# Attention, a dense layer and eight experts in one kernel: the last routing by halves and pairs, conversions behind the selection, contiguous copies of transposed queries and keys

## The chip, the cores and the metric

The kernel runs on one core of a Trainium2 chip. The time is the device time of one execution in microseconds, as the median of several runs. The profile is one execution recorded by the hardware profiler; times in it count from the first instruction of the core.

## The reference

Three stages follow one another: causal attention with a window of 64, a dense layer with a gated activation, and eight experts of which each token takes at most one.

```python
def reference(...):
    # attention: q, k, v of (4, 8, 576, 64); rel = query - key position
    scores = where((rel >= 0) & (rel < 64), q @ k.T / sqrt(64), -1e9)
    attn = softmax(scores) @ v
    x = attn.transpose(0, 2, 1, 3).reshape(2304, 512)
    # dense layer, w_in 512 x 2048, w_out 2048 x 512
    h = x @ w_in
    x = (h * tanh(softplus(h))) @ w_out
    # experts: 8, w1 512 x 1024, w2 1024 x 512
    keep = x @ w_skip > 0
    logits = x @ w_gate
    e = argmax(logits); gate = softmax(logits)[e]
    y = gate * (relu(x @ w1[e]) @ w2[e])
    return where(keep, x + y, x)
```

## The kernel before

The 2304 tokens are six blocks (`m`) of 384, each three tiles (`t`) of 128. The program has two parts, and in each a planner (`Plan`) orders tasks by costs, due times and buffer counts that are written into the code, and then emits them; within such a region every engine issues in the order of emission. `rounds` is emitted at the end of the first region, behind all its tasks. Where the instructions of one region fall among those of the other on the same engine is left to a scheduler.

The first part does the attention in 24 pairs of heads (`pr`), the dense layer in 96 chunks (`L1`, activation, `L2`), and the routing of each block. For the first eight pairs queries and keys are loaded in their natural layout, four rows to a partition, and transposed on TensorE (`nat_T`, line 437) into PSUM; `nat_k` and `nat_q` copy them to SBUF (helper `copy`, lines 317 on ScalarE and 319 on VectorE), with a step of four words in what they write.

The routing of a tile: `xe` copies the tile out of PSUM and negates it (lines 830, 832), `rT` transposes it (843), `re` copies the transposes, `rl` forms the logits (873), and a `Group` of tiles goes through some 15 small VectorE instructions: maximum, one-hot, the place among the tokens of an expert (`place` on TensorE), the row in the experts' buffer (`keep`, line 946), sum, gate, tag, and the running count `cum`. Blocks 0 to 4 form a group of three tiles; the last block has three groups of one. `scatter` then writes the tokens to the experts' rows in DRAM.

For the last block expert 0 doesn't wait for DRAM: `pick_mat` (line 1093) makes a selection matrix of 0 and 1 from the rows, `select` (1099) multiplies it with the tile split in two parts (`xs_H`, `xs_L`), and `sel_H` copies the selected tokens of each half of the features to SBUF (`xgH`). `rounds` (1147 to 1160) then computes from the counts the value `nrounds` and, for each expert, `level`, which says how many of its places are taken.

In the second part TensorE does for each expert `E1` in four steps (`fp`, line 1222) with two PSUM buffers, which `h_H` (1249) and `h_L` (1255, VectorE) read, then `E2` (1266), between its steps the transposes of the next expert's tokens (`xg_T`, 1208), and at the end `E2_second`. Before the fourth step of `E1` TensorE reads `level` into a register (`load_over`). SyncE reads `nrounds` (line 1432, at the end of the code).

The weights of the experts' second layer are loaded as f32 (`el`, line 333) and split into a rounded part (`eH`, a cast) and a remainder (`eL`, line 343, a subtraction on VectorE). The first 32 weight tiles are handled in the first part, as the dense weights in their places are used up; their staging buffers (`cv`) are two. The last four of the 32 are tiles j = 4 to 7 of expert 2. `keep_warm` (1176) fills TensorE's planned waits in the first part with matmuls without use.

Of the kernel before, what the change touches and what calls it, by code (L numbers as in the profile page):

```python
# [9 lines left out]
F32 = mybir.dt.float32  # L10
# [12 lines left out]
N1 = 144  # L23
# [148 lines left out]
def tile_kernel(  # L172
# [37 lines left out]
    def ctile(shape, dt, name):  # L210
        return cst.tile(shape, dt, tag=name, name=name)
# [42 lines left out]
    G.iota(iota8, pattern=[[NE, CAP]], base=0, channel_multiplier=0)  # L254
    first_t = []
    for n in (1, 1, 1, 3):
        t = ctile([128, n, NE + 1], F32, f"first{len(first_t)}")
        G.memset(t, 0.5)
        first_t.append(t)
    nslot = [0]  # L260
# [80 lines left out]
    def expert_L(eng, key):  # L341
# [21 lines left out]
    BUFS = dict(ps=3, ph=2, po0=1, po1=1, po2=1, rk=4, rq=2, vt=3, kT=2, qT=2, P=2, PT=2, xHL=2,  # L363
                cv=2, ca=2, u=3, gHL=2, xs=3, xf=1, grp3=1, grp1=3, lqs=1)
    plan = Plan(BUFS)
# [63 lines left out]
    def nat_T(pr, i):  # L429
        t = nat[pr][i]  # L430
        nr = nat[pr][2] if i else 96
        if pr < 4:
            o = ps_o.tile([128, 4, 128], F32, tag=f"po{i}", name="tqk")
        else:
            o = ps_s.tile([128, 4, 128], F32, tag="ps", name="tqk")
# [391 lines left out]
    def x_evac(eng, m, t):  # L827
# [6 lines left out]
        G.tensor_copy(xs[:, DM + 1:XW].bitcast(I32), tok[:, n:n + 1])  # L834

    def x_store(m, t):
        n = 3 * m + t
        SP.dma_start(out=out[128 * n:128 * n + 128, :], in_=xs_t[m, t][:, :DM])
# [6 lines left out]
    def route_Te(eng, m, t):  # L845
        if m == NB - 1:
            xf = rqp.tile([128, NK, 128], F32, tag="rk", name="xf", bufs=4)
        else:
            xf = sml.tile([128, NK, 128], F32, tag="xf", name="xf", bufs=1)
        copy(eng, xf, xf_t[m, t])  # L850
        xf_t[m, t] = xf

    def route_few(m, t):
# [16 lines left out]
    def route_lg(m, t):  # L870
        lp_t[m, t] = lp = ps_s.tile([128, NE + 1], F32, tag="ps", name="lp")
        for kk in range(NK):
            PE.matmul(lp, xf_t[m, t][:, kk], wgs[:, kk, :NE + 1], start=kk == 0, stop=kk == NK - 1)
# [5 lines left out]
    class Group:  # L879


        def __init__(self, m, t0, n):
            self.m, self.t0, self.n, self.i = m, t0, n, 3 * m + t0

        def lg(self):
            if self.n == 1:
                return lp_t[self.m, self.t0].rearrange("p (n c) -> p n c", n=1)
            return lg_t[self.m]

# [3 lines left out]
        def small(self, w, name, dt=F32):  # L893
            return sml.tile([128, self.n, w], dt, tag=f"{name}{self.n}", name=name, bufs=3 if self.n == 1 else 1)

# [17 lines left out]
        def first(self):  # L913
            self.f = first_t[self.t0 if self.n == 1 else 3]
            V.scalar_tensor_tensor(self.f[:, :, :NE], self.z, 0.0, self.d, op0=ALU.is_ge, op1=ALU.mult)
# [81 lines left out]
    for m in range(NB):  # L997
# [3 lines left out]
        for t in range(3):  # L1001
            T(("xe", m, t), two(.48, .6), lambda e, m=m, t=t: x_evac(e, m, t), after=[("L2t", NF * m + NF - 1, t) if last else ("L2", NF * m + NF - 1)],
              get=[("xs", ("xs", m, t))], use=[("po", m, t)], due=tb + 2)
            T(("xo", m, t), one(SS, .45), lambda e, m=m, t=t: x_store(m, t), after=[("xe", m, t)], lat=2.5,
              due=tb + 20, use=[("xs", m, t)])
            T(("rT", m, t), one(PP, .43), lambda e, m=m, t=t: route_T(m, t), after=[("xe", m, t)] + [("re", m, t - 1)] * (t > 0),
              get=[("ps", ("rtp", m, t))], due=tb + dt * (2 + 2 * t), use=[("xs", m, t)])
            T(("re", m, t), two(.48, .6), lambda e, m=m, t=t: route_Te(e, m, t), after=[("rT", m, t)],
              get=[("rk" if last else "xf", ("xf", m, t))], use=[("rtp", m, t)])
            if not last:  # L1010
# [4 lines left out]
                continue  # L1015
            T(("rl", m, t), one(PP, .75), lambda e, m=m, t=t: route_lg(m, t), after=[("re", m, t), ("wg",)],
              get=[("ps", ("lp", m, t))], use=[("xf", m, t)], due=tb + dt * (3 + 2 * t))
# [4 lines left out]
        prev = None  # L1022
        for t0, n in ([(t, 1) for t in range(3)] if last else [(0, 3)]):
            g = Group(m, t0, n)
            lgs = [("lg", m) if n > 1 else ("rl", m, t0)]
            lu = [("lp", m, t0)] if n == 1 else []
            key = lambda x, m=m, t0=t0: (x, m, t0)
# [3 lines left out]
            def R(name, eng, cost, fn, after, use=(), late=0.0, get=(), lat=None, g=g, gb=gb, td=td):  # L1031
# [21 lines left out]
            for t in range(n):  # L1053
# [60 lines left out]
    for t in range(3):  # L1114
        T(("sH", t), two(.52, .34), lambda e, t=t: xs_H(e, t), after=[("xe", L, t)],
          get=[("xHL", "xsHL")] if t == 0 else (), use=[("xs", L, t)], due=te + 10 + t, behind=[("sH", t - 1)] * (t > 0))
        T(("sL", t), one(VV, .6), lambda e, t=t: xs_L(e, t), after=[("sH", t)], use=[("xs", L, t)],
          due=te + 12 + t)
        T(("pm", t), one(VV, .2), lambda e, t=t: pick_mat(t), after=[("ke", L, t)], get=[("kT", ("pick", t))] if t != 1 else (), use=[("pick", 0)] if t == 1 else (),
          behind=[("pm", t - 1)] * (t > 0), due=te - 3 + .1 * t)  # L1120
# [12 lines left out]
    for n in range(32):  # L1133
# [3 lines left out]
        if key[1] < NK:  # L1137
# [79 lines left out]
    def E1(e, fp):  # L1217
        ph_t[e, fp] = ph = pl1.tile([128, 2, N1], F32, tag="ph2", name="ph2")
        for i in range(2):
            f = 2 * fp + i  # L1220
            for kk in range(NK):
                PE.matmul(ph[:, i], w1_t[e, kk][:, 128 * f:128 * f + 128], xgT[e][:, kk, :N1],  # L1222
                          start=kk == 0, stop=kk == NK - 1)

# [241 lines left out]
```

## Time and profile before

| | us |
|---|---|
| median of 3 runs | 688.57 (687.44 to 689.02) |
| the profiled execution, its own time | 686.42 |
| its span, first to last instruction | 684.60 |
| TensorE busy (matmuls) | 669.3 |
| VectorE busy | 460.5 |
| ScalarE busy | 410.2 |
| GpSimd busy | 60.0 |

The engines are PE (TensorE; PEld its weight loads), DVE (VectorE), ACT (ScalarE), POOL (GpSimd) and SP (SyncE; SPq its issues). A matmul's end is modelled, so a busy TensorE is not one at its peak, and the matmuls of `keep_warm` count as busy. A row of a timeline gives the start in us, the duration in us, engine, line, operation, output<-inputs, shape and count, and in brackets how long the engine was idle before and what released it. A row of a window gives the stretch, its length, the busy us (and instructions) of PE, PEld, DVE, ACT and POOL, the granted TensorE clock as a share of 2.4 GHz, the busy share of the DMA engines, and GB/s. A row of a group gives line, engine, operation, shapes and count, then the busy us and the mean ns of one, then the idle time before. Loads are told by the minimum, median and maximum time from issue to landing in us.

### The profile page before, as it was taken

How to read it: one execution, taken by the hardware profiler on the slowest of the kernel's cores; microseconds unless marked ns; L12 is line 12 of the kernel's file. 1: busy time of each engine (PE TensorE's matmuls, PEld its weight loads, DVE VectorE, ACT ScalarE, POOL GpSimd, SP SyncE). 2: the span in 40 equal slices, each digit the busy share in tenths (PEclk: the TensorE clock that was granted, in tenths of full speed). 3: DMA queues.
4: the chain of work that ended last, by engine and by line, in shares of the span. 5: the costliest groups of instructions: out<-in, count | busy, mean ns of one | idle time of the engine just before them, and what ended most of it. 6: DMA issues, size and time to landing. Idle time of an engine off the chain costs nothing. (4 is left out here: it accounts for less than half of the span.)

```text
span 684.6 us, 13449 instructions
## 1 busy us (share of the span) xinstructions
PE 669.3 (98%) x4870; PEld 574.7 (84%) x4870; DVE 460.5 (67%) x1298; ACT 410.2 (60%) x994; POOL 60.0 (9%) x114
## 2 busy tenths in 40 slices
PE   7999999999999999999999999999999999999995
PEld 6787766788888888988888888898888888998983
DVE  4999999876666555565776656566678574685352
ACT  5999778677667775776555565456554253543241
POOL 3000000000010001000020001100020122211141
PEclk9999999999999999999999999999999999999998
DMA  9999966877432312232220100044564677588300
GB/s 203 284 323 315 245 128 135 200 152 158 78 75 46 81 35 56 47 93 50 51 60 13 58 1 11 18 152 139 155 178 167 227 255 249 208 281 294 142 18 28
DMA packets 150493, 92.54 MB, mean 135 GB/s; under 512 B 111869, under 2 KB 128253, under 8 KB 150416
## 3 DMA queue, kind: packets, MB, share of 16 engines
q1 hardware_dynamic: 147696, 87.11, 47.1%
q0 software_dynamic: 2720, 4.42, 1.7%
q8 instruction: 46, 0.75, 0.5%
q14 instruction: 31, 0.25, 0.1%
HBM read 73.96 MB, written 17.86 MB: 134 GB/s over the span
## 5 line engine op out<-in xcount | busy, mean ns | idle before, releaser
L737 PE MATMUL ph<-xH,w 128*128 128x384 f32 x768 | 220.6, 348 | 0.2
L788 PE MATMUL po<-w,gH 128*128 128x512 f32 x480 | 154.3, 402 | 0.0
L737 PEld LDWEIGHTS ph<-xH,w 128*128 128x128 f32 x768 | 140.9, 188 | 7.0 <-issue 1.7
L737 PE MATMUL ph<-xL,w 128*128 128x384 f32 x384 | 130.0, 338 | 0.0
L745 ACT ACTIVATE u<-u 128x384 f32<-128x384 f32 x96 | 50.3, 524 | 121.2 <-DVE u L742 121.2
L788 PEld LDWEIGHTS po<-w,gH 128*128 128x128 f32 x480 | 87.2, 188 | 17.2 <-issue 1.6
L788 PE MATMUL po<-w,gL 128*128 128x512 f32 x240 | 95.0, 396 | 0.0
L764 DVE SCALAR_TENSOR_TENSOR u<-u,ph 128x384 f32<-128x384 f32 x80 | 44.1, 551 | 68.0 <-ACT u L758 67.6
L737 PEld LDWEIGHTS ph<-xL,w 128*128 128x128 f32 x384 | 72.2, 188 | 4.0 <-issue 2.2
L1222 PEld LDWEIGHTS ph<-xgT,w 128*128 128x128 f32 x512 | 63.9, 190 | 1.5 <-DVE xgT L319 0.4
L1222 PE MATMUL ph<-xgT,w 128*128 128x144 f32 x512 | 64.7, 287 | 0.4 <-DVE xgT L319 0.3
L742 DVE TENSOR_SCALAR u<-ph 128x384 f32<-128x384 f32 x96 | 53.2, 554 | 14.8 <-PE ph L737 13.7
L773 DVE TENSOR_TENSOR gL<-u,gH 128x384 fp32r<-128x384 f32 x80 | 44.5, 557 | 17.1 <-ACT gH L317 14.2
L531 ACT ACTIVATE P<-P,mx 128x128 f32<-128x128 f32 x144 | 55.6, 390 | 0.1
L788 PEld LDWEIGHTS po<-w,gL 128*128 128x128 f32 x240 | 45.1, 188 | 10.8
L749 ACT ACTIVATE u<-u 128x384 f32<-128x384 f32 x96 | 50.4, 525 | 2.9
L758 ACT ACTIVATE u<-u 128x384 f32<-128x384 f32 x96 | 50.2, 523 | 2.3
L755 ACT ACTIVATE u<-u 128x384 f32<-128x384 f32 x96 | 50.1, 522 | 2.3
L788 PE MATMUL po<-w,g 128*128 128x512 f32 x96 | 44.0, 594 | 0.0
L343 DVE TENSOR_TENSOR w<-st,w 128x512 fp32r<-128x512 f32 x64 | 42.6, 683 | 0.6
L1266 PE MATMUL po<-w,hH 128*128 128x512 f32 x128 | 42.6, 414 | 0.0
L279 POOL DMA_INDIRECT xg_d<-xs,r_si x18 | 18.6, 1031 | 234.4 <-DVE gH L319 74.3
(166 smaller groups left out, 966.8 us busy)
## 6 DMA issues: line engine op xcount, KB each, us to landing
st<-in_moe_w_dram SPq DMA_DIRECT2D x64, 256.0 KB, 5.9
w<-in_moe_w_dram SPq DMA_DIRECT2D x32, 512.0 KB, 5.2
w<-in_moe_w_in_dram SPq DMA_DIRECT2D x16, 512.0 KB, 6.3
w<-in_moe_w_out_dram SPq DMA_DIRECT2D x16, 512.0 KB, 6.3
out_dram<-xs SPq DMA_DIRECT2D x18, 256.0 KB, 2.4
xg<-xg_d SPq DMA_DIRECT2D x16, 257.0 KB, 3.8
ca<-w SPq DMA_DIRECT2D x16, 256.0 KB, 3.2
xg_d<-nothing SPq DMA_DIRECT2D x16, 256.0 KB, 4.9
```

Of the source, the lines that this page charges most:

```text
L343: eng.tensor_tensor(l, raw_w.pop(key), h.bitcast(F32), op=ALU.subtract)
L531: A.activation(P[:, i], P[:, i], AF.Exp, bias=mx[:, 0, u % 2, i:i + 1], scale=-1.0, accum_out=mx[:, 1, u % 2, i:i + 1])
L737: PE.matmul(phs[c], a[:, kk], b[:, kk], start=kk == 0 and n == 0, stop=kk == NK - 1 and n == len(terms) - 1)
L742: V.tensor_scalar(u, phs[c], 20.0, None, op0=ALU.min)
L745: A.activation(us[c], us[c], AF.Exp)
L749: A.activation(us[c], us[c], AF.Square, bias=1.0)
L755: A.activation(us[c], us[c], AF.Ln, scale=0.5, bias=half_t[c])
L758: A.activation(us[c], us[c], AF.Exp, scale=-1.0)
L764: V.scalar_tensor_tensor(o, us[c], 1.0, phs[c], op0=ALU.subtract, op1=ALU.mult)
L773: eng.tensor_tensor(gL, us[c], gH.bitcast(F32), op=ALU.subtract)
L788: PE.matmul(po[m, t], a[:, ts], b, start=f == 0 and n == 0, stop=f == NF - 1 and n == len(terms) - 1)
L1222: PE.matmul(ph[:, i], w1_t[e, kk][:, 128 * f:128 * f + 128], xgT[e][:, kk, :N1], start=kk == 0, stop=kk == NK - 1)
```

## The change

Four things change. The transposes of queries and keys are written to PSUM with a step of four words, so that the copies out of it are contiguous on both sides. In the last block the third tile's two copies (`xe`, `re`) are split into a half on VectorE and a half on ScalarE. Tiles 0 and 1 of that block are routed as a group of two, tile 2 as a group of one, whose places count the first group's one-hot rows directly and so don't wait for `cum`. Other work is ordered behind: `sl`, `sm` (and with it `ep`, `ga`, `tg`) and `co` behind the last selection matrix, `sL` of tiles 1 and 2 behind the third tile's copies, and `eH` of expert 2's tiles behind both selection copies, which are now fixed to one on ScalarE and one on VectorE. The first step of `E1` of expert 0 goes through the first half of the features for both outputs before the second.

```diff
-    for n in (1, 1, 1, 3):
+    for n in (1, 2, 3):
...
-            o = ps_o.tile([128, 4, 128], F32, tag=f"po{i}", name="tqk")
+            o = ps_o.tile([128, 128, 4], F32, tag=f"po{i}", name="tqk")
...
-            PE.transpose(o[:, r, :nr], t[:nr, r].rearrange("p j d -> p (j d)"), ident[:nr, :nr])
+            PE.transpose(o[:, :nr, r], t[:nr, r].rearrange("p j d -> p (j d)"), ident[:nr, :nr])
...
-            copy(eng, kT[:, c0 + pad:c0 + pad + nk].rearrange("p (a r) -> p r a", r=4), tqk[pr, 1][:, :, r0:r0 + nk // 4])
+            copy(eng, kT[:, c0 + pad:c0 + pad + nk], tqk[pr, 1][:, r0:r0 + nk // 4].rearrange("p a r -> p (a r)"))
...
-        copy(eng, qk_tiles(pr)[0].rearrange("p (a r) -> p r a", r=4), tqk[pr, 0][:, :, :96])
+        copy(eng, qk_tiles(pr)[0], tqk[pr, 0][:, :96].rearrange("p a r -> p (a r)"))
...
+    def x_evac_half(eng, m, t, n):
...
+        hs = slice(256 * n, 256 * n + 256)
+        if eng is A:
+            A.activation(xs_t[m, t][:, hs], po[m, t][:, hs], AF.Copy, scale=-1.0)
+        else:
+            V.tensor_scalar(xs_t[m, t][:, hs], po[m, t][:, hs], -1.0, None, op0=ALU.mult)
...
+    def route_Te_half(eng, m, t, n):
...
+        copy(eng, xf[:, 2 * n:2 * n + 2], p[:, 2 * n:2 * n + 2])
...
-                for t2 in range(t):
-                    PE.matmul(pp[:, t], ones8, self.oh[:, t2], start=False, stop=False)
+                for o in self.front + [self.oh[:, t2] for t2 in range(t)]:
+                    PE.matmul(pp[:, t], ones8, o, start=False, stop=False)
...
+            if halves:
+                T(("re", m, t), one(VV, .3), lambda e, m=m, t=t: route_Te_half(e, m, t, 0), after=[("rT", m, t)],
+                  get=[("rk", ("xf", m, t))], use=[("rtp", m, t)])
+                T(("re2", m, t), one(AA, .3), lambda e, m=m, t=t: route_Te_half(e, m, t, 1), after=[("rT", m, t)],
+                  behind=[("re", m, t)], use=[("rtp", m, t)])
...
-        for t0, n in ([(t, 1) for t in range(3)] if last else [(0, 3)]):
-            g = Group(m, t0, n)
+        for t0, n in ([(0, 2), (2, 1)] if last else [(0, 3)]):
+            g = Group(m, t0, n, g)
...
-            R("pl", PP, .1, Group.place, [key("oh")] + ([prev("co")] if prev else [("co", m - 1, 0)] if m else []),
-              get=[("ps", ("pp", m, t0))])
+            R("pl", PP, .1, Group.place, [key("oh")] + ([prev("oh")] if prev else [("co", m - 1, 0)] if m else []),
+              get=[("ps", ("pp", m, t0))], use=[("grp", m, 0)] * (t0 > 0))
...
-            R("sl", VV, .07, Group.slot, [key("ro")], (), .5)
+            R("sl", VV, .07, Group.slot, [key("ro")] + [("pm", 2)] * last, (), .5)
...
-            R("sm", VV, .1, Group.sum, [key("se")], (), .5)
+            calm = [("pm", 2)] * last
+            R("sm", VV, .1, Group.sum, [key("se")] + calm, (), .5)
...
-            R("co", VV, .21 * n, Group.count, [key("pl")], (), 1)
+            R("co", VV, .21 * n, Group.count, [key("pl")] + calm + ([prev("co"), key("pl")] if prev else [("pl", m, 2)] * last), (), 1)
...
-        T(("sL", t), one(VV, .6), lambda e, t=t: xs_L(e, t), after=[("sH", t)], use=[("xs", L, t)],
+        T(("sL", t), one(VV, .6), lambda e, t=t: xs_L(e, t), after=[("sH", t)] + [("xe", L, 2)] * (t == 1) + [("re", L, 2)] * (t == 2), use=[("xs", L, t)],
...
-        T(("xgH", i), two(.52, .6), lambda e, i=i: sel_H(e, i), after=[("se2", t, i) for t in range(3)],
+        T(("xgH", i), one(VV if i else AA, .55), lambda e, i=i: sel_H(e, i), after=[("se2", t, i) for t in range(3)],
...
-        T(("eH", key), two(.52, .34), lambda e, key=key, i=i: expert_H(e, key, i), after=[("el", key), last_use[i]],
+        T(("eH", key), two(.52, .34), lambda e, key=key, i=i: expert_H(e, key, i), after=[("el", key), last_use[i]] + [("xgH", 0), ("xgH", 1)] * (key[0] > 1),
...
+        if e == 0 and fp == 0:
+            order = [(i, kk) for k2 in (0, 2) for i in range(2) for kk in (k2, k2 + 1)]
+        else:
+            order = [(i, kk) for i in range(2) for kk in range(NK)]
```

## Rows read from the trace of the kernel before

**Rows 1.** Windows; columns as told above:

```profile
24.00:28.00 4.00, 3.34 (x56) 3.09 (x56) 3.53 (x17) 3.20 (x12) 0.29 (x2) 1.00 1.08 331
...
40.00:60.00 20.00, 19.68 (x137) 13.95 (x135) 19.41 (x50) 18.19 (x44) 0.35 (x2) 1.00 1.12 291
...
560.00:660.00 100.00, 100.00 (x677) 89.98 (x677) 53.75 (x95) 40.79 (x78) 15.02 (x11) 1.00 0.62 220
```

**Rows 2.** Timeline of TensorE at the hand-over; columns as told above:

```profile
529.60 0.39 PE L1099 MATMUL sel<-pick,xsH 128*128 128x256 f32 x1
...
531.75 0.56 PE L1176 MATMUL warm<-ones 128*128 128x128 bf16 x7
...
532.12 0.37 PE L1099 MATMUL sel<-pick,xsH 128*128 128x256 f32 x1
...
533.63 8.22 PE L1222 MATMUL ph<-xgT,w 128*128 128x144 f32 x64 [0.29 <-DVE xgT L319]
...
541.59 0.72 PE L1266 MATMUL po<-w,hH 128*128 128x512 f32 x2
...
544.95 0.61 PE L1208 MATMUL tp<-ident,xg 128*128 128x128 f32 x4
```

**Rows 3.** VectorE's timeline, routing's end to the selection copies:

```profile
530.84 0.15 DVE L946 TENSOR_SCALAR row_all<-r_r 128x1 f32<-128x1 f32 x1
...
530.96 0.68 DVE L343 TENSOR_TENSOR w<-st,w 128x512 fp32r<-128x512 f32 x1
...
531.56 0.35 DVE L1093 TENSOR_SCALAR pick<-iota,row_all 128x256 fp32r<-128x256 int16 x1
...
532.88 1.29 DVE L319 COPY xgT<-sel 128x512 f32<-128x512 f32 x2 [0.97 <-PE sel L1099]
```

**Rows 4.** Groups by form, whole run; columns as told above:

```profile
L317 ACT ACTIVATE kT<-tqk 128x384 f32<-128x384 f32 x4 | 3.5, 871 | 1.8 <-PE tqk L437 1.8
...
L317 ACT ACTIVATE PT<-tp 128x384 f32<-128x384 f32 x31 | 14.1, 483 | 3.5 <-PE tp L552 3.4
...
L319 DVE CAST w<-st 128x512 fp32r<-128x512 f32 x28 | 11.6, 423 | 13.8 <-PE po L788 8.0 <-DMA st<-in_moe_w_dram 5.2 <-PE ph2b L1236 0.6
...
L437 PE MATMUL tqk<-ident,nq 96*128 96x96 f32 x32 | 4.0, 247 | 0.4 <-DMA nq<-in_q_dram 0.4
```

**Rows 5.** VectorE's timeline in the head:

```profile
14.91 0.43 DVE L652 TENSOR_SCALAR cv<-w 128x512 int32<-128x512 int32 x1 [1.44 <-DMA w<-in_moe_w_in_dram]
```

**Rows 6.** Timeline of the last expert's end:

```profile
676.21 0.68 ACT L1303 ACTIVATE yf<-po,folded 64x512 f32<-64x512 f32 x1 [4.70 <-PE po L1296]
...
676.92 0.76 DVE L1309 SCALAR_TENSOR_TENSOR y<-po,xg 64x512 f32<-64x512 f32 x1 [3.71 <-ACTq L1433]
```

**Rows 7.** Timeline of SyncE's DMA issues at the hand-over:

```profile
515.40 2.79 SPq L333 DMA_DIRECT2D st<-in_moe_w_dram  x2
...
537.62 0.43 SPq L1200 DMA_DIRECT2D xg<-xg_d  x1
```

**Rows 8.** The tile st, 485 to 500 us, its loads:

```profile
DMA to landing us min/median/max: 2.6/2.7/2.9
```

**Rows 9.** VectorE's timeline after the selection copies:

```profile
534.09 0.16 DVE L1151 TENSOR_REDUCE mc<-cp 128x1 f32<-128x8 f32 x1
...
535.28 0.17 DVE L1159 SCALAR_TENSOR_TENSOR level<-cp,th 128x8 int32<-128x8 f32 x1
...
536.49 0.46 DVE L1255 SCALAR_TENSOR_TENSOR hL<-ph,hH 128x288 fp32r<-128x288 f32 x1 [0.97 <-ACT hH L1249]
```

**Rows 10.** Instructions of line 1432: durations in ns, first and last start:

```profile
L1432 SPq TENSOR_LOAD <-nrounds x1: 484/484/484, 535.0 to 535.0; - x1
```

**Rows 11.** The tile xg, its load issued at 537.62:

```profile
DMA to landing us min/median/max: 5.0/5.0/5.0
```

**Rows 12.** Windows at and after TensorE's last matmul:

```profile
676.00:677.00 1.00, 0.17 (x1) 0.00 (x0) 0.08 (x1) 0.68 (x1) 0.00 (x0) 1.00 0.06 16
...
681.00:682.00 1.00, 0.00 (x0) 0.00 (x0) 0.00 (x0) 0.00 (x0) 0.00 (x0) 0.50 0.07 13
```

More of the change, by code (lines that the diff above doesn't have):

```diff
@@ L870, in route_lg @@
     def route_lg(m, t):
[L871 removed]
+        if t != 1:
+            lp_t[m, t] = ps_s.tile([128, 2 - t // 2, NE + 1], F32, tag="ps", name="lp")
+        lp = lp_t[m, t - t % 2][:, t % 2]
         for kk in range(NK):
@@ L879, in tile_kernel, with __init__, front @@
     class Group:
-        def __init__(self, m, t0, n):
-            self.m, self.t0, self.n, self.i = m, t0, n, 3 * m + t0
+        def __init__(self, m, t0, n, prev=None):
+            self.m, self.t0, self.n, self.i, self.prev = m, t0, n, 3 * m + t0, prev
+        @property
+        def front(self):
+            return [self.prev.oh[:, t] for t in range(self.prev.n)] if self.prev else []
         def lg(self):
-            if self.n == 1:
-                return lp_t[self.m, self.t0].rearrange("p (n c) -> p n c", n=1)
-            return lg_t[self.m]
+            return lg_t[self.m] if self.n == 3 else lp_t[self.m, self.t0]
         def bc(self, ap):
@@ L893, in small @@
         def small(self, w, name, dt=F32):
-            return sml.tile([128, self.n, w], dt, tag=f"{name}{self.n}", name=name, bufs=3 if self.n == 1 else 1)
+            return sml.tile([128, self.n, w], dt, tag=f"{name}{self.n}", name=name, bufs=1)
         def max1(self):
@@ L1001, in tile_kernel @@
         for t in range(3):
-            T(("xe", m, t), two(.48, .6), lambda e, m=m, t=t: x_evac(e, m, t), after=[("L2t", NF * m + NF - 1, t) if last else ("L2", NF * m + NF - 1)],
-              get=[("xs", ("xs", m, t))], use=[("po", m, t)], due=tb + 2)
-            T(("xo", m, t), one(SS, .45), lambda e, m=m, t=t: x_store(m, t), after=[("xe", m, t)], lat=2.5,
+            halves = last and t == 2
+            done = [("L2t", NF * m + NF - 1, t) if last else ("L2", NF * m + NF - 1)]
+            if halves:
+                T(("xe", m, t), one(VV, .3), lambda e, m=m, t=t: x_evac_half(e, m, t, 0), after=done,
+                  get=[("xs", ("xs", m, t))], use=[("po", m, t)], due=tb + 2)
+                T(("xe2", m, t), one(AA, .3), lambda e, m=m, t=t: x_evac_half(e, m, t, 1), after=done,
+                  behind=[("xe", m, t)], use=[("po", m, t)], due=tb + 2)
+            else:
+                T(("xe", m, t), two(.48, .6), lambda e, m=m, t=t: x_evac(e, m, t), after=done,
+                  get=[("xs", ("xs", m, t))], use=[("po", m, t)], due=tb + 2)
@@ L1005, in tile_kernel @@
+            xe = [("xe", m, t)] + [("xe2", m, t)] * halves
+            T(("xo", m, t), one(SS, .45), lambda e, m=m, t=t: x_store(m, t), after=xe, lat=2.5,
               due=tb + 20, use=[("xs", m, t)])
[L1006 removed]
+            T(("rT", m, t), one(PP, .43), lambda e, m=m, t=t: route_T(m, t), after=xe + [("re", m, t - 1)] * (t > 0),
               get=[("ps", ("rtp", m, t))], due=tb + dt * (2 + 2 * t), use=[("xs", m, t)])
[L1008 to L1009 removed]
+            if halves:
+                T(("re", m, t), one(VV, .3), lambda e, m=m, t=t: route_Te_half(e, m, t, 0), after=[("rT", m, t)],
+                  get=[("rk", ("xf", m, t))], use=[("rtp", m, t)])
+                T(("re2", m, t), one(AA, .3), lambda e, m=m, t=t: route_Te_half(e, m, t, 1), after=[("rT", m, t)],
+                  behind=[("re", m, t)], use=[("rtp", m, t)])
+            else:
+                T(("re", m, t), two(.48, .6), lambda e, m=m, t=t: route_Te(e, m, t), after=[("rT", m, t)],
+                  get=[("rk" if last else "xf", ("xf", m, t))], use=[("rtp", m, t)])
@@ L1015, in tile_kernel @@
                 continue
-            T(("rl", m, t), one(PP, .75), lambda e, m=m, t=t: route_lg(m, t), after=[("re", m, t), ("wg",)],
-              get=[("ps", ("lp", m, t))], use=[("xf", m, t)], due=tb + dt * (3 + 2 * t))
+            T(("rl", m, t), one(PP, .75), lambda e, m=m, t=t: route_lg(m, t), after=[("re", m, t), ("wg",)] + [("re2", m, t)] * halves,
+              get=[("ps", ("lp", m, t))] * (t != 1), use=[("xf", m, t)] + [("lp", m, 0)] * (t == 1), due=tb + dt * (3 + 2 * t))
         if not last:
@@ L1021, in tile_kernel @@
             T(("lg", m), one(VV, .1), lambda e, m=m: route_lge(m), after=[("rs", m)], use=[("lp", m)])
-        prev = None
-        for t0, n in ([(t, 1) for t in range(3)] if last else [(0, 3)]):
-            g = Group(m, t0, n)
-            lgs = [("lg", m) if n > 1 else ("rl", m, t0)]
-            lu = [("lp", m, t0)] if n == 1 else []
+        prev = g = None
+        for t0, n in ([(0, 2), (2, 1)] if last else [(0, 3)]):
+            g = Group(m, t0, n, g)
+            lgs = [("rl", m, t0 + t) for t in range(n)] if last else [("lg", m)]
+            lu = [("lp", m, t0)] if last else []
             key = lambda x, m=m, t0=t0: (x, m, t0)
@@ L1218, in E1 @@
         ph_t[e, fp] = ph = pl1.tile([128, 2, N1], F32, tag="ph2", name="ph2")
-        for i in range(2):
+        if e == 0 and fp == 0:
+            order = [(i, kk) for k2 in (0, 2) for i in range(2) for kk in (k2, k2 + 1)]
+        else:
+            order = [(i, kk) for i in range(2) for kk in range(NK)]
+        for i, kk in order:
             f = 2 * fp + i
-            for kk in range(NK):
-                PE.matmul(ph[:, i], w1_t[e, kk][:, 128 * f:128 * f + 128], xgT[e][:, kk, :N1],
-                          start=kk == 0, stop=kk == NK - 1)
+            PE.matmul(ph[:, i], w1_t[e, kk][:, 128 * f:128 * f + 128], xgT[e][:, kk, :N1],
+                      start=(i, kk) == order[0], stop=(i, kk) == order[-1])
     def E1_second(e, fq):
```

23 lines of the change are left out of this document (15 added, 8 removed).

## The prediction

> **What bounds the kernel now.** I read the busy time by stage first. From about 40 us to the end of the experts TensorE has no idle time to speak of: 19.68 of 20 us at 40 to 60, 100.00 of 100 in the experts [rows 1]. So a stage that TensorE fills gives nothing for faster copies; what counts is a place where TensorE waits, or is made to wait. Two places are touched. The first is the head, before 40 us, where VectorE is the fullest engine (3.53 of 4 us at 24 to 28 [rows 1]). The second is the hand-over from the last block's routing to the first expert, read instruction by instruction in the timelines of TensorE [rows 2] and VectorE [rows 3]: selection matmuls, a pause before the last tile's eight of them (531.63 to 532.12), copies, E1 of expert 0 at 533.63, its E2 at 541.59, the transposes for expert 1 at 544.95. Call S the start of the last tile's selection (532.12) and T the end of the second selection copy (532.88 + 1.29 = 534.17).
>
> **The copies of queries and keys.** A ScalarE copy of 128x384 that writes every fourth word took 871 ns, a contiguous one 483 ns [rows 4]. So each such copy becomes up to 0.4 us shorter. What is that worth? Pairs 4 to 7 lie beyond 40 us, where TensorE is full: nothing. For pairs 0 to 3 the chain to the first score matmuls shortens by some 0.4 us a pair, but VectorE then stands in its queue before a weight conversion that waits for its DMA until 14.91 [rows 5], and that DMA does not move; after it VectorE is nearly dense (0.47 us idle at 24 to 28). Bounds 0 to 0.6 us, taken 0.2, nearer the lower end because the DMA absorbs what comes before it. One memset fewer on GpSimd is nothing: it lies behind the loads at the start.
>
> TensorE now writes these transposes to PSUM with a step of four words. No row shows such a write. Lower bound: 0, as the number of columns is the same. Upper bound by the nearest row, ScalarE's price for that step, 871/483 = 1.8: the 32 query transposes took 4.0 us busy [rows 4], so all 64 about 8, and 0.8 x 8 = 6.5 us more, half of it (pairs 4 to 7) where TensorE is full: 3.2 us. I take 0, the matmul engine being another than the one that paid. The Trainium skill, "SBUF — State Buffer", section "Door 1: The DMA port swizzle", speaks against this edit: it says that any non-contiguous access pattern in PSUM slows matmuls significantly. By that rule the sum would be up to the 3.2 us worse; it is a rival below, and no run here shows it yet.
>
> **The last tile by halves.** The two halves of `xe` and of `re` read one PSUM bank from two engines. The end of the trace shows such a pair [rows 6]: y of L1309 needs nothing from yf, yet VectorE starts it at 676.92, just when ScalarE's read of the same bank ends (676.21 + 0.68 = 676.89). So I expect the halves one after the other, and no gain; TensorE is filled at that time with the logits of tiles 0 and 1 anyway. Bounds 0 to 0.3 us gained, taken 0.
>
> **Two tiles as a group, small work behind the selection.** Before, VectorE put a 0.68 us weight subtraction (530.96) between the last tile's row and its selection matrix, which came at 531.56 [rows 3], and TensorE paused. Without it the matrix can come 0.6 us earlier. The grouping takes some 14 small instructions out of VectorE's queue, but tile 0 now waits for tile 1's logits, so the first selection stays near 529.5. Its first 16 matmuls took 529.60 to 531.75 [rows 2]; so TensorE itself allows S of about 531.4. Gain 0.7 (bounds 0 and 1.2). The sums, gates, tags and counts that now come after the last matrix, some 14 at 0.06 to 0.07 us from start to start (two of them lie between 530.84 and 530.96), about 1 us, fit into VectorE's wait for the selection; GpSimd's scatters begin about 0.6 us later relative to S, and the loads that need them come 8 us after. One copy on each engine and E1's new order: E1 of the first pair waited only from 533.63 plus four of its 64 matmuls (4/64 of 7.96 us, 0.5) to 534.17: at most 0.2, taken 0.1. Sum of the gains here: 0.8 us. T was S + 2.05 and becomes about 531.4 + 1.95 = 533.3.
>
> **The cost: four weight conversions behind the selection.** Expert 2's tiles j = 4 to 7 now have `eH` behind both selection copies. `cv` has two buffers. Two tiles are staged before, and the other two can only be loaded when `eL` of the first two is done; before, this took place while the last chunks were multiplied (loads issued from 515.40 on [rows 7]) and was hidden. Now all of it lies after T, in the queue of VectorE, in front of `rounds` (written out in the same ordered region) and the first `hL`:
> - two casts of 0.42 and two subtractions of 0.68, somewhat overlapped: the first subtraction ends at T + 1.4, the second at T + 2.0 [rows 3, 4];
> - the loads of 256 KB land 2.6 to 2.9 us after issue [rows 8]: T + 4.1 and T + 4.8;
> - cast, subtract, cast, subtract: T + 6.4.
>
> What is late next? `rounds` begins at T + 6.3 instead of at 534.09, right at T. Three waits follow it.
> 1. `level` came 1.2 us after its start (535.28 [rows 9]) and must be in a TensorE register before E1's last quarter: T + 7.7, and 0.5 to 0.9 for the load (484 ns on SyncE [rows 10], and its checks), T + 8.4. A quarter of E1 is 1.96 us; from its last one to the transposes of expert 1 it was 544.95 - (541.59 - 1.96) = 5.3 us. Transposes at T + 13.7 = 547.0.
> 2. SyncE reads `nrounds` before the experts' loads (535.0 [rows 10]), and the first row load of expert 1 followed 2.6 us later (537.62 [rows 7]), landing 5.0 us on [rows 11]. So T + 6.3 + 0.9 + 2.6 + 5.0 = T + 14.8 = 548.1.
> 3. If VectorE keeps the written order, `hL` of E1's first quarter also waits for `rounds`: T + 7.8 + 0.46 (its duration, 536.49 [rows 9]). E1 has two PSUM buffers, so its third quarter starts at T + 8.25, and the transposes come at T + 8.25 + 7.3 = T + 15.5 = 548.8. If ready instructions of the expert region may pass (as SyncE's `nrounds` load did, which stands at the end of the code), this wait is not there.
>
> Before, the transposes were at 544.95. So the later waits give +3.2 (no. 2) or +3.9 us (no. 3), the gains of 0.8 already being in T. TensorE is full from there on, so nothing is given back. With 0.2 from the head: +3.0 to +3.7. I take +3.2. Bounds: no. 3 with S not earlier and nothing from the head, 3.9 + 0.7 = +4.6; wait 1 alone (+2.1), with conversions that begin on ScalarE right after its own copy, about 1 us sooner, and the head's 0.2, +0.9.
>
> The profiled execution took 686.42 us (span 684.60, and 1.82 around it), 0.3% under the median 688.57. The sum puts it at 689.6, and the median at 688.57 + 3.2 = 691.8.
>
> **Rivals.**
> - *The conversions stay covered (faster).* TensorE reaches E1's last quarter about 5.4 us after T; if the value of `level` is there by then and the row loads are too, only the gains remain: 0.8 + 0.2, with up to 0.5 more from the group, 687.1. It decides from the point where the second pair of conversions ends before about T + 3.3. For it: VectorE and ScalarE have little else to do during E1. Against it: one load alone lands no earlier than 2.6 us after a subtraction that ends at T + 1.1 at best. 0.12.
> - *Stall and gain about equal* (one of the two loads staged before, so that a single conversion chain is left; stall about 1.5 us): 688 to 689.9. 0.13.
> - *TensorE's clock falls in the stall.* In case no. 3 TensorE is idle from 536.8 to 541.6, 4.7 us. At the end of the trace its last matmul ended at 676.17 with the clock at 1.00, and the granted clock was 0.50, the 1.2 GHz level, from 681 [rows 12]. A resumed E1 would run its last two quarters (3.9 us) at half rate in part: up to 3.9 us more, about 2 as it looks, 694. The Trainium skill, "TensorE: Matmul & The Clock Gate", section "HAM oscillation", warns that an idle gap in mid-kernel makes the following work start at half rate; by it the sum would be this rival's. 0.06.
> - *The strided PSUM writes are slow.* 0 to 3.2 us on top, about 693. 0.07.
> - The forecast: 0.62.
>
> **Numbers.** A measurement of this kernel tells about 0.2% (1.4 us) from no change. Slower: forecast, clock and PSUM, 0.75, less 0.03 for the forecast's lower edge: 0.72. Same: 0.13 + 0.03 = 0.16. Faster: 0.12. The range must leave out no more than 0.2: the faster case (0.12) and the clock's (0.06) are out; from the equal case's 688.4 to 694.2, which takes in the upper bound of the forecast whole (688.57 + 4.6 = 693.2).
>
> **What the profile after would show.** Right: `eH`, `eL` of four tiles on VectorE or ScalarE behind the selection copies, two 256 KB loads between them, `rounds` some 6 us after T, SyncE's `nrounds` load with it, and an idle TensorE of 3 to 5 us in E1 or before the transposes of expert 1, which come at about 548 (shifted by the head's gain). S at 531 to 531.6, halves not overlapping, query and key copies of 0.5 us. The prediction is wrong if `rounds` runs right after T, if TensorE has no wait longer than 1 us between 533 and 550, or if the head moves by more than a microsecond.

## The result and the profile after

The changed kernel took 694.95 us in the median of 4 runs (693.56 to 695.73), the kernel before 688.30 beside it; the ratio is 1.0092 with a 95% interval of 1.0074 to 1.0109. Five more rounds of runs (experiment 12) gave 1.0094 (1.0071 to 1.0117). So the change costs 0.92%, 6.3 us, where 3.2 were forecast. The profiled execution took 695.64 us with a span of 693.9, 9.3 more than the span of before. That is more than the medians' difference because the profiled execution of before lay 2.2 us under its median; a second profile of before, below, has a span of 686.2 and sets 7.7 against the same 693.9.

TensorE's timeline after, at the hand-over; it answers to [rows 2]:

```profile
530.73 0.56 PE L1137 MATMUL sel<-pick,xsH 128*128 128x256 f32 x1
...
534.59 6.15 PE L1263 MATMUL ph<-xgT,w 128*128 128x144 f32 x48 [0.20 <-ACT xgT L316]
544.20 2.22 PE L1263 MATMUL ph<-xgT,w 128*128 128x144 f32 x16 [3.47 <-DVE folded L1198]
...
551.75 0.65 PE L1246 MATMUL tp<-ident,xg 128*128 128x128 f32 x4 [2.09 <-DMA xg<-xg_d]
...
595.66 4.19 PE L1263 MATMUL ph<-xgT,w 128*128 128x144 f32 x32 [0.70 <-DVE hL L1296]
```

Before, E1 of expert 0 ran its 64 matmuls without a break [rows 2]. Now it stops after 48 of them for 3.47 us, released by the last instruction of `rounds`; then TensorE waits 2.09 us more for the rows of expert 1, and 0.70 us later on for an `hL`. Against the first profile of before its matmuls are 0.96 us later at E1's start, 4.48 at E1's last quarter (539.72 before), 6.80 at the transposes.

VectorE's timeline after, from the second selection copy on; it answers to [rows 9]:

```profile
534.40 0.69 DVE L318 COPY xgT<-sel 128x512 f32<-128x512 f32 x1 [1.78 <-PE sel L1137]
535.01 0.76 DVE L318 CAST w<-st 128x512 fp32r<-128x512 f32 x2
535.69 1.28 DVE L342 TENSOR_TENSOR w<-st,w 128x512 fp32r<-128x512 f32 x2
537.35 0.46 DVE L1296 SCALAR_TENSOR_TENSOR hL<-ph,hH 128x288 fp32r<-128x288 f32 x1 [0.38 <-ACT hH L1290]
539.30 0.43 DVE L318 CAST w<-st 128x512 fp32r<-128x512 f32 x1 [1.50 <-DMA st<-in_moe_w_dram]
...
541.07 0.69 DVE L342 TENSOR_TENSOR w<-st,w 128x512 fp32r<-128x512 f32 x1
541.68 0.16 DVE L1189 TENSOR_REDUCE mc<-cp 128x1 f32<-128x8 f32 x1
...
543.10 0.17 DVE L1197 SCALAR_TENSOR_TENSOR level<-cp,th 128x8 int32<-128x8 f32 x1
```

This is the forecast chain: two tiles converted, a wait for the DMA of the other two, two more conversions, and only then `rounds`. T, the end of the second selection copy, is 534.40 + 0.69 = 535.09; `rounds` begins at T + 6.6. One thing was left open and is settled: `hL` of the first quarter, an instruction of the other ordered region, passes at 537.35, so forecast wait 3 is not there. Waits 1 (`level`) and 2 (the row loads) both are.

SyncE's queue after, the issues, and its read of `nrounds`; they answer to [rows 7] and [rows 10]:

```profile
536.39 8.97 SPq L332 DMA_DIRECT2D st<-in_moe_w_dram  x5
545.41 2.83 SPq L1238 DMA_DIRECT2D xg<-xg_d  x6
```

```profile
L1473 SPq TENSOR_LOAD <-nrounds x1: 485/485/485, 542.8 to 542.8; - x1
```

The row loads went out at 545.41 instead of 537.62 [rows 7], 2.6 us after `nrounds`, as before, and the transposes could start 6.3 us after the first issue (551.75 - 545.41), where I had reckoned with 5.0 [rows 11]. The view of the tile xg for these six loads, and who waited for them, tells why:

```profile
L1238 SPq DMA_DIRECT2D xg<-xg_d x6: 430/432/442, 545.4 to 547.8; - x6
...
  PE tp L1246: 2.1, 1
...
DMA to landing us min/median/max: 4.7/5.4/6.9
```

Load by load, the view names the transposes (`tp`) as waiting only for the third, issued at 546.37: the first two bring the rows of expert 0. So the time is two more issues (0.96) and a landing of 5.3.

The clock in windows of the changed kernel:

```profile
18.00:20.00 2.00, 2.00 (x31) 1.57 (x28) 1.01 (x2) 1.30 (x7) 0.00 (x0) 0.50 0.87 151
...
530.00:532.00 2.00, 2.00 (x19) 2.00 (x16) 1.91 (x15) 0.00 (x0) 0.00 (x0) 0.50 0.00 0
...
540.00:544.00 4.00, 0.74 (x7) 0.52 (x5) 3.17 (x14) 0.41 (x1) 0.00 (x0) 1.00 0.00 0
...
552.00:554.00 2.00, 2.00 (x9) 1.67 (x8) 1.14 (x3) 1.50 (x3) 0.00 (x0) 0.62 1.05 395
554.00:556.00 2.00, 2.00 (x8) 1.60 (x8) 0.00 (x0) 0.44 (x2) 0.00 (x0) 0.52 1.06 403
```

Three stretches ran at 1.2 GHz: in the head behind an idle time of 2.89 us, through the routing and the first selection matmuls, and for about 3 us behind the wait for rows, where E2 lost another 1.6 us (6.80 late at 551.75, 8.4 at the next expert's E1, 557.28).

The copies and the halves, by form and in the timelines of VectorE and ScalarE; the first fence answers to [rows 4]:

```profile
L436 PE MATMUL tqk<-ident,nq 96*128 96x96 f32 x32 | 4.0, 247 | 0.0
...
L316 ACT ACTIVATE kT<-tqk 128x384 f32<-128x384 f32 x4 | 1.9, 486 | 2.0 <-PE tqk L436 2.0
```

```profile
525.03 0.42 DVE L843 TENSOR_SCALAR xs<-po 128x256 f32<-128x256 f32 x1 [0.29 <-PE po L787]
```

```profile
525.49 0.38 ACT L841 ACTIVATE xs<-po 128x256 f32<-128x256 f32 x1 [1.32 <-DVE xs L843]
```

The transposes take 247 ns with a step of four words in PSUM, as without it, and the copy of 128x384 fell from 871 to 486 ns. The second half of `xe` begins at 525.49, when the first ends (525.03 + 0.42 = 525.45): one after the other, as forecast. The row names VectorE's copy as what released ScalarE; whether the bank or the program's own order asks for that was not separated.

### The profile page after: what moved, and what is told of

Same layout as the page of the kernel before. It is cut to its first block, busy times and chain, and to the rows that moved or that the text cites. A ratio compares the mean times of both kernels' runs of the same rounds, so it can differ in the third digit from the quotient of the medians.

```text
span 693.9 us, 13427 instructions
## 1 busy us (share of the span) xinstructions
PE 673.3 (97%) x4866; PEld 578.5 (83%) x4866; DVE 460.2 (66%) x1287; ACT 405.1 (58%) x993; POOL 54.4 (8%) x113
```

## The experiments

Ratios are against the kernel before, run beside each; 1% is 6.9 us. The first four take the change apart.

**1. Everything but the conversions behind the selection.**

```
-  after=[("el", key), last_use[i]] + [("xgH", 0), ("xgH", 1)] * (key[0] > 1)
+  after=[("el", key), last_use[i]]
```

> The changed kernel, with expert 2's four conversions (j = 4 to 7) no longer put behind the selection copies; all else as changed. Theory (order): the conversions behind the selection cost E1's late last quarter (3.5 us idle), the late transposes of expert 1 (2.1 us) and the half rate after them (1.5 us), so the kernel loses 6 to 7 us, to 687.5 to 689.5, and TensorE has no wait over 1 us between 534 and 552. Rival (selection and clock): what lies ahead of the first expert, the selection at half rate at 529 to 532 and the head, costs most; then this run stays above 692.

Measured: 690.58 us, ratio 1.0021 (1.0006 to 1.0035); 4.9 us less than the changed kernel (1.0092 - 1.0021 = 0.71%), where I had expected 6 to 7. The break in E1 is gone. What is left is on TensorE and GpSimd:

```profile
534.67 8.11 PE L1263 MATMUL ph<-xgT,w 128*128 128x144 f32 x64 [0.20 <-ACT xgT L316]
...
546.79 0.66 PE L1246 MATMUL tp<-ident,xg 128*128 128x128 f32 x4 [0.76 <-DMA xg<-xg_d]
...
620.38 4.19 PE L1263 MATMUL ph<-xgT,w 128*128 128x144 f32 x32 [1.11 <-DVE hL L1296]
```

```profile
534.34 0.98 POOL L278 DMA_INDIRECT xg_d<-xs,r_si  x1 [23.65 <-DVE xs L982]
```

The order of the conversions is the main cost. The rest is no clock effect, as the granted clock did not fall in this profile ahead of the kernel's end. The scatters, which started at 530.77 in the first profile of before, start 3.6 us later, and the row loads with them; 1.0 us of that was there ahead of the last routing (0.5 in the second profile of before).

**2. The kernel before with the conversions behind the selection alone.** The edit of 1, the other way round.

> The kernel before, with only this added: expert 2's four conversions behind both selection copies. Theory (order): the weight loads' round trip, rounds, level and the row loads come late as in the changed kernel; 6 to 7 us slower, 694 to 696, and E1's last quarter after an idle of 3 us or more. Rival (the other parts matter): without the group and the new order of the selection the conversions find room; at most 3 us slower, 688 to 691.5. My forecast's own sum for this edit (3.2 and the 0.8 that offsets it) gives +4.0, 692.5.

Measured: 696.85 us, ratio 1.0112 (1.0092 to 1.0133), +7.7 us, above the range of either theory. Within the noise this one edit does as much harm alone as the whole change; TensorE waits 4.13 us ahead of E1's last quarter and 1.43 ahead of the transposes. My sum's +4.0 for it was too small.

**3 and 4. The contiguous copies taken out of the changed kernel, and put into the one before.** The edit of 4 is shown; that of 3 is its reverse, and the copy of the keys changes with it.

```
-  o = ps_o.tile([128, 4, 128], F32, tag=f"po{i}", name="tqk")
-  PE.transpose(o[:, r, :nr], ...)
...
-  copy(eng, qk_tiles(pr)[0].rearrange("p (a r) -> p r a", r=4), tqk[pr, 0][:, :, :96])
+  o = ps_o.tile([128, 128, 4], F32, tag=f"po{i}", name="tqk")
+  PE.transpose(o[:, :nr, r], ...)
...
+  copy(eng, qk_tiles(pr)[0], tqk[pr, 0][:, :96].rearrange("p a r -> p (a r)"))
```

> The changed kernel with the old copies and transposes of queries and keys (the copies write every fourth word, the transposes write contiguously). Theory (head): the new copies made TensorE's first stage start 0.4 to 0.7 us earlier and then cost it 0.6 us net, by a longer wait for the weight DMA and a stretch at half rate at 16 to 20 us; with the old ones the head is back and the kernel is 0.6 us faster than the changed one, within 0.2% of it. Rival 1: the copies are a gain and the loss in the head comes from elsewhere (other memsets, other plan): 0.4 us or more slower. Rival 2: transposes that write with a step cost in pairs 4 to 7 too: up to 3 us faster.

> The kernel before with the contiguous copies of queries and keys alone. Theory (head): between 0.2 us faster and 0.8 us slower, with a granted clock below 1.00 at 16 to 20 us. Rival 1 (the copies gain): 0.4 to 0.7 us faster, clock 1.00 at 16 to 20 us. Rival 2 (stepped PSUM writes are slow): 3 us slower, transposes clearly above 247 ns.

Measured: without them the changed kernel takes 695.90 us, 1.0100 (1.0081 to 1.0119); with them the kernel before takes 688.27, 0.9988 (0.9973 to 1.0003). Both differences point to a gain of 0.5 to 0.8 us, neither is surely more than nothing; a loss in the head, my theory here, is not borne out. It stood on one profile against a fast one.

**5. Experiment 1, and the small work no longer behind the last selection matrix.**

```
-  R("sl", ..., [key("ro")] + [("pm", 2)] * last, ...)
...
-  calm = [("pm", 2)] * last
+  R("sl", ..., [key("ro")], ...)
...
+  calm = []
```

> The changed kernel without the conversions behind the selection, and now also without the small work behind the last selection matrix (slots, sums, counts free to run earlier, as before); groups, halves, copies and E1's order stay. Without this edit the scatters ran at 534.3 to 537.9 us and TensorE waited 0.76 us for the row loads and 0.5 and 1.1 us for hL later. Theory (scatters): slots and gates come 1.5 to 3 us earlier, the scatters with them, those waits go, and the kernel is 1.4 to 2.4 us faster than with the small work behind, 688 to 689. Rival (selection): the small work now stands ahead of the selection matrices, the selection starts 0.5 us or more later, and the time stays or grows (690.5 or more).

Measured: 688.59 us, 0.9998 (0.9981 to 1.0014), 1.6 us less than experiment 1 (0.23%, little more than the noise of the two). The first scatter starts at 531.56, and the waits for rows and for the first late `hL` are gone; one of 1.22 us at 618.48 stays. So the late scatters are the second cost, by the waits that went with them rather than by the ratio alone. My forecast had them 0.6 us later relative to S "and the loads that need them come 8 us after". In experiment 1 SyncE's queue, with `nrounds` long there, went on 1.75 us after the last scatter's end (537.88 to 539.63), and in experiment 8 1.76 us after it; in the first profile of before, where `nrounds` came last, it went on 1.95 us after that end (534.31 to 536.26). So there were 0.2 us to spare, not 8.

Three runs ask what in the conversions costs: that `rounds` stands behind them, or the round trip to DRAM between them.

**6. `rounds` ahead of the conversions**, which stay behind the selection.

```
+  told = []
   def expert_H(eng, key, i):
+      if key == (2, 4) and not told:
+          told.append(rounds())
...
   plan.emit(keep_warm)
-  rounds()
```

> The changed kernel, complete, with the call of rounds written ahead of expert 2's first conversion and so still behind the selection copies. Theory 1 (the order of rounds): level and nrounds come 1.3 us after the copies; E1's last quarter, the SyncE read and the row loads are no longer late; the 3.5 us of idle and most of the transposes' delay go; 689.5 to 691. Theory 2 (the conversions themselves): the weight loads that wait for conversions stand in SyncE's queue ahead of the row loads, and these stay late; 0 to 3.5 us faster than the changed kernel, 691.5 to 694.5.

Measured: 694.96 us, 1.0094 (1.0072 to 1.0116): nothing gained, and above the range of either theory. SyncE's issues and TensorE's timeline:

```profile
537.69 7.11 SPq L332 DMA_DIRECT2D st<-in_moe_w_dram  x5
544.85 2.80 SPq L1241 DMA_DIRECT2D xg<-xg_d  x6
```

```profile
534.54 8.34 PE L1266 MATMUL ph<-xgT,w 128*128 128x144 f32 x64 [0.20 <-ACT xgT L316]
...
550.76 1.12 PE L1249 MATMUL tp<-ident,xg 128*128 128x128 f32 x4 [4.62 <-DMA xg<-xg_d]
```

E1 runs through, and most of the stall (4.62 of 5.56 us) comes back ahead of the transposes; the clock fell in that wait, and the next expert's E1 is 8.0 us later than in the first profile of before, against 8.4 in the changed kernel. `nrounds` was there at 535.84, but SyncE now waited until 542.9 for the last `eL` (ended at 542.12 + 0.68 = 542.80) before it issued the weight loads of the second part, and the row loads stand behind those. The two waits of the forecast were one behind the other in front of the same queue; with either alone TensorE is as late.

**7. Four staging buffers**, so that all four tiles are loaded ahead of the selection.

```
+  tag = "ca" if key in ((2, 6), (2, 7)) else stg[1]
-  get=[("cv", ("st", key))]
+  get=[("ca" if key in ((2, 6), (2, 7)) else "cv", ("st", key))]
```

> The changed kernel, complete, but the last two of the four weight tiles are loaded into two other staging buffers, so that all four are staged ahead of the selection and no load lies between the conversions. Theory (round trip): the conversions end 3 us sooner (about 3.5 us after the selection copies instead of 6.4), rounds with them; the wait of 3.5 us shrinks to 1 or less, and the row loads come 3 us sooner; 689.5 to 692. Rival (the conversions' own work on VectorE sets rounds): less than 1 us faster, 694 or more.

Measured: 693.58 us, 1.0066 (1.0045 to 1.0088), 1.8 us less than the changed kernel, between my theory's range and the rival's; the two intervals overlap. The conversions end at 537.40, 3.1 us after that kernel's T, the wait in E1 is 0.26 us, but `nrounds` comes at 539.0, the row loads go out from 541.63 on, and the transposes, 7.1 us later, still wait 2.84 us.

**9 and 10. Both repairs together; and both with the small work of 5.**

> The changed kernel with both repairs: all four weight tiles staged ahead of the selection (two more staging buffers) and rounds ahead of the conversions, which still stand behind the selection copies. Theory (row loads): E1 has no wait, but the row loads of expert 1 are still held, by the last scatter (about 537.2) and the last conversion (about 539.5); they are issued at 540.5 to 541.6 instead of 541.6 with four buffers alone and 545.4 in the changed kernel, and TensorE still waits 1.5 to 3 us ahead of the transposes: 692 to 693.6. Rival (level): the wait for level was the true cost and with both repairs all of it is gone: 690.5 or less.

> As the kernel with both repairs (all four tiles staged ahead, rounds ahead of the conversions), and the small work no longer behind the last selection matrix, so that the scatters start about 2 us sooner. Theory (two holders of the row loads): without the late scatters only the conversions hold them; 0.5 to 1.5 us faster than with the two repairs alone, 691 to 692.5, and the transposes of expert 1 still wait for the row loads. Rival: the scatters do not matter as long as conversions come after the selection; the same time as with the two repairs.

Measured: 690.42 us, 1.0025 (1.0011 to 1.0039), and 690.09 us, 1.0018 (1.0004 to 1.0032). Each repair alone gave 0 and 1.8 us, both together 4.6 (0.67%). My theory of a wait for rows of 1.5 to 3 us failed, and the rival's 690.5 or less came: the rows are there in time. What is left, in experiment 9, on VectorE and TensorE:

```profile
537.17 2.49 DVE L347 TENSOR_TENSOR w<-st,w 128x512 fp32r<-128x512 f32 x4
539.58 0.82 DVE L1300 SCALAR_TENSOR_TENSOR hL<-ph,hH 128x288 fp32r<-128x288 f32 x2
```

```profile
540.09 4.19 PE L1267 MATMUL ph<-xgT,w 128*128 128x144 f32 x32 [1.29 <-DVE hL L1300]
```

Now the four conversions hold `hL`, and E1 waits 1.29 us for a PSUM buffer: the conversions' own work, which before lay under the dense layer. With that wait there, earlier scatters bring nothing that can be measured.

**8. The edits of the hand-over that put nothing late**, in the kernel before with the contiguous copies: one selection copy on each engine, E1's new order, and the one weight subtraction ahead of the last selection matrix put behind it.

```
-  T(("xgH", i), two(.52, .6), ...)
+  T(("xgH", i), one(VV if i else AA, .55), ...)
...
-  after=[("eH", key)], ...
+  after=[("eH", key)] + [("pm", 2)] * (key == (2, 7)), ...
```

> The kernel before with the contiguous copies and three of the change's edits at the hand-over, none of which puts conversions or scatters later: one selection copy on VectorE and one on ScalarE, E1's first pair in the new order, and the one weight subtraction that stood ahead of the last selection matrix put behind it. Theory: the 0.49 us pause of TensorE goes, and 0.2 to 0.6 us of the copies; 0.5 to 0.9 us on top of the copies' 0.8: 687.2 to 688.2. Rival: another wait takes their place (the second copy, or loads of expert 1): as with the copies alone, 688.3 to 689.

Measured: 687.80 us, 0.9977 (0.9963 to 0.9992): faster than both kernels, though not surely faster than the copies alone (experiment 4, 0.9988). VectorE's timeline shows the subtraction in what was a wait:

```profile
531.82 0.35 DVE L1093 TENSOR_SCALAR pick<-iota,row_all 128x256 fp32r<-128x256 int16 x1
532.09 0.69 DVE L343 TENSOR_TENSOR w<-st,w 128x512 fp32r<-128x512 f32 x1
533.69 0.69 DVE L319 COPY xgT<-sel 128x512 f32<-128x512 f32 x1 [0.91 <-PE cp L1149]
```

T is 534.38, 0.4 us ahead of the second profile of before, and TensorE does its 24 selection matmuls with no pause.

**11 and 12. Second profiles of the kernel before and of the changed one.**

> The kernel before, a second profiled execution, to tell what of the differences between two profiles is spread between executions. If the first one (686.42 us, clock 1.00 at 16 to 20 us) was at the lower end, this one has its first expert's E1 and its transposes 0.5 to 2 us later, in step with a later head, and no new wait of TensorE between 533 and 560 us. If instead its hand-over lies where the first one's did, within 0.3 us, the head's shift of 0.6 us belongs to the change.

> The changed kernel, a second profiled execution and five more rounds, to tell which of its losses belong to the order and which to one execution. Theory: the waits of 3 to 4 us ahead of E1's last quarter and of 1.5 to 2.5 us ahead of expert 1's transposes are there again, since queues set them, and the time is 693.5 to 696; of the granted clock's three falls (head, selection, after the row loads) at least one is absent, since the kernels with the same parts show them only in some profiles. Rival: all three falls are there at the same places, and so are part of the change's price.

Measured: before, one execution of 688.02 us, span 686.2: the first expert's E1 is at 534.14 and everything from the head to its transposes 0.5 to 0.6 us later than in the first profile. So the 0.6 us that the changed kernel's matmuls were late from 60 to 520 us in its first profile lie within the spread; in its second profile they were 1.9 us late, which the two profiles of before don't cover. After: 695.43 us in the median, span 692.5 in the profile:

```profile
531.86 0.39 PE L1137 MATMUL sel<-pick,xsH 128*128 128x256 f32 x1 [0.25 <-DVE pick L1131]
535.15 6.15 PE L1263 MATMUL ph<-xgT,w 128*128 128x144 f32 x48 [0.20 <-ACT xgT L316]
544.64 3.78 PE L1263 MATMUL ph<-xgT,w 128*128 128x144 f32 x16 [3.34 <-DVE folded L1198]
552.37 0.66 PE L1246 MATMUL tp<-ident,xg 128*128 128x128 f32 x4 [0.58 <-DMA xg<-xg_d]
```

The wait in E1 is there again. This time the clock fell behind it (E1's last quarter took 3.78 us instead of 2.22), and the wait for rows shrank to 0.58: the half rate ate time that TensorE would have waited anyway. The transposes are 6.8 us later than in the second profile of before, against 6.2 in the first profile after. The fall at the selection is absent.

## Why the prediction was right in kind and wrong in size

**The mechanism is the forecast one.** Conversions with a round trip to DRAM, then `rounds`, then `level`, `nrounds` and the row loads; experiments 1 and 2 give it 4.9 and 7.7 us of a total of 6.3. What failed are sizes: the gain ahead of T, the chain from T to the transposes of expert 1, and two terms taken as next to nothing, the clock and later waits. Profiled executions are compared here, first with first and second with second. How late each one already was is read from the transposes of the last block's tile 1, in TensorE's timelines of the first and second profile of before, then the first and second after:

```profile
524.24 0.60 PE L843 MATMUL rtp<-ident,xs 128*128 128x128 f32 x4
...
524.74 0.60 PE L843 MATMUL rtp<-ident,xs 128*128 128x128 f32 x4
...
524.77 0.60 PE L852 MATMUL rtp<-ident,xs 128*128 128x128 f32 x4
...
526.15 0.60 PE L852 MATMUL rtp<-ident,xs 128*128 128x128 f32 x4
```

1. *T.* Forecast 533.3, 0.87 earlier than 534.17; measured 535.09, 0.92 later, and again 0.88 later in the second pair (534.97 + 0.69 = 535.66 against 533.39 + 1.39 = 534.78). Counted from those transposes, T came after 9.93 and 10.04 us before, and after 10.32 and 9.51 in the changed kernel. The 10.32 is the profile in which the clock stood at half rate through the routing; the 9.51 is without that fall, and experiments 3, 6 and 7, with the same order and no fall there, have 9.51 as well. So the edits did bring T forward at full clock, by 0.42 us against the first profile of before, not by 0.87. The step that failed is "so the first selection stays near 529.5": at full clock it came 5.71 us after the transposes instead of 5.36. A group of two passes its small instructions only when the logits of both tiles are there; TensorE then does 24 selection matmuls in one piece, 3.3 us from the first to E1 (531.86 to 535.15) instead of 4.0 (529.60 to 533.63). Experiment 8 removes the pause without the group, and T comes after 9.34. Error in the first pair: 1.8 us, of which 0.45 is the gain, 0.8 the clock at the routing, and 0.5 was there ahead of the last routing, as in the second profile of before.
2. *The chain from T to the transposes.* Forecast T + 14.8, measured T + 16.66 and T + 16.7. `rounds` began at T + 6.6 instead of 6.3; its own 0.9 became 1.1, as an `hL` slipped in between; from `nrounds` to the first issue it was 2.6 as forecast; then 6.3 us instead of 5.0, since I took the load at 537.62 for that of expert 1 and it is expert 0's: the one that TensorE needs is the third, and landed in 5.3 us (from its issue to the transposes it was 5.0 in experiment 6 and 6.2 in experiment 7). Error: 1.9 us, in both pairs.
3. *The clock.* I gave the fall in the stall 0.06, with "about 2 as it looks". It fell in both profiles after, at other places each time: at the routing (in term 1) and behind the wait for rows, 1.6 us lost, in one; behind the wait in E1 in the other, 1.56, of which the shorter wait for rows gave most back.
4. *Later waits.* 0.7 us at 595.66 for an `hL`, in the sum nothing. Others were 1.11 us in experiment 1, 1.22 in 5, 0.94 in 8 at 587.74, none above 0.2 in either profile of before or the second after. VectorE's queue ahead of the late `hL` had waited for a weight load, until 591.26 in the changed kernel; that these waits come and go with the landing of such loads is my reading.

1.8 + 1.9 + 1.6 + 0.7 on top of 3.2 make 9.2 of the 9.3 us by which the first profile after exceeds the first of before. In the medians 3.1 us are missing (6.3 against 3.2). The two errors that both pairs show, the gain (0.45) and the chain (1.9), make 2.3 of them; the rest is left to the clock and to late waits, which differ from one execution to the next.

**Right.** The copies' durations, 871 to 486 ns, and a small gain (0.2 forecast, 0.5 to 0.8 measured, not surely above nothing). The stepped PSUM writes at nothing: 247 ns with and without. The Trainium skill, "SBUF — State Buffer", section "Door 1: The DMA port swizzle", says that non-contiguous PSUM access slows matmuls significantly. These transposes, which write 96 or 112 words to a partition with a step of four, show no sign of it (the same 247 ns), and here the measurement decides. The halves one after the other. The forecast that either wait, 1 or 2, would do: in experiment 6 wait 1 is gone, most of the stall stands at wait 2, and the time is the same.

**The rivals.** The conversions are not covered: even with all tiles staged and `rounds` ahead (experiment 9) E1 waits 1.29 us. The "equal" case is not this kernel; that experiment, with both loads staged, comes near it (690.42, 1.0025). The clock's rival came true in part, on top of the forecast. PSUM did not.

**Open.** The group itself was not run alone. Experiment 5 (group, halves, copies, E1's order) against 4 (copies) gives +0.10%, 0.7 us, with intervals that overlap; that it costs nothing is not excluded. The profiles show no gain from it either: from tile 1's transposes to T it was 9.96 us in experiment 5, 9.94 in 4, and 9.34 in 8, which has neither group nor halves. Why SyncE's first load of the second part waits for the last `eL` was only read from the two times (542.80 and 542.9; 539.66 and 539.80 in experiment 9); that the second part's staging buffers lie where the first part's were is my reading.

## What to carry to other kernels

Before work is put behind a point because "the engine is idle there", list every queue in which something now stands behind it: here VectorE (`rounds`, `hL`), TensorE (`level`) and SyncE (`nrounds`, the staging buffers, and behind them the rows of the next expert). Two waits in front of the same consumer hide each other, so a repair of one can measure as nothing (0 and 1.8 us) and the two together as 4.6. When tiles are grouped to save small instructions, ask first when the group's last input arrives: the first result moves to that time, here by 0.35 us. Before a shift between two profiles is put down to a change, count from an event ahead of the place that was changed.

## What the runs showed of the hardware

- The clock after an idle TensorE is not decided by the idle time alone. Idle times of 3.47 us (the changed kernel, 540.7 to 544.2) and 2.84 us (experiment 7) left it at 1.00. After 4.13 (experiment 2) and 4.62 us (experiment 6) windows of 2 us stood at 0.50, after 3.34 us (second profile after) a stretch of 4 us at a mean of 0.64, after 3.25 us (experiment 3) two windows at 0.60 and 0.55; and after 2.09 us, 7.5 us behind the end of the wait of 3.47, it was 0.62 and 0.52 in the changed kernel. The Trainium skill, "TensorE: Matmul & The Clock Gate", section "HAM oscillation — how this bites in real kernels", tells of half rate after waits for data. The trace agrees in so far as half rate follows most of these waits. One more fall came at the routing (528 to 532 us in the changed kernel and in experiments 9 and 10), where TensorE was busy 2.00 of 2.00 us in each window, with narrow matmuls of 9 columns and those of `keep_warm`; it came in 3 of the 9 profiles with the new routing and in none of the 5 with the old one.
- In the head the clock fell in 7 of 10 profiles with contiguous copies and in none of 4 with the old ones, in the changed kernel behind an idle time of 2.89 us (1.78 in the first profile of before). VectorE waited there for the weight DMA, 2.55 us until 15.34 (before 1.44 until 14.91 [rows 5]): shorter copies end earlier, and the DMA does not. That the falls belong to the copies is not shown: the four executions with the old ones that were profiled were each faster than the median of their kernel's runs, two of them the fastest of six, and the medians of experiments 3 and 4 show no loss by the copies.
